# A transformer block on one core: the second half's x turned in 32x32 blocks on VectorE instead of by TensorE

## The chip, the cores and the metric

One core of a Trainium2 chip runs the whole program. The metric is the device time in microseconds (us), median of several runs. Everything is in 32-bit floats; TensorE multiplies in its float32r form, and each operand is split into a high part and a low remainder, so that one product is three matmuls (high x high, high x low, low x high).

## The reference

```python
x = A_x                                          # [1, 2048, 1024]
h = x + _A_ref(_layernorm(x), A_wqkv, A_w_phi, A_wo)
h2 = h + _B_ref(_layernorm(h), B_w1, B_w2)       # relu MLP, 1024 -> 3584 -> 1024

def _A_ref(x, wqkv, w_phi, wo):                  # 32 heads of 32
    q, k, v = ...                                # x @ wqkv, cut into heads
    pq = einsum("bhsd,hdf->bhsf", q, w_phi);  pk = einsum("bhsd,hdf->bhsf", k, w_phi)
    phi_q = concat([softmax(pq), softmax(-pq)]); phi_k = concat([softmax(pk), softmax(-pk)])
    kv = einsum("bhsf,bhsd->bhfd", phi_k, v);  z = phi_k summed over s
    o = (phi_q @ kv) / (phi_q @ z + 1e-6)
    return o @ wo
```

## The kernel before

**Tiles and halves.** The 2048 tokens are 16 tiles of 128, in two halves of eight (HT = 8). In a first part the weight w_phi is folded into the q and k weights; the folded weights are stored in DRAM as `wpk` (k, four sets of 256 columns) and `wpq` (q, two sets of 512 columns). Then comes a list of items, in an order that is the order of TensorE. An item is one tile against one set of weights: eight steps, one for each block of 128 input features, three matmuls of 512 columns a step. For each half the list has four kv slabs (set s = 0 to 3, each over eight tiles; columns are 256 of folded k and 256 of v) and then two q slabs (set s = 0 and 1, eight tiles each). After the second half follow attention, the output projection, and the MLP by a scheme with seven products for eight.

**x in its turned form.** For an item TensorE needs the normalised x with features on the partitions. A tile is held as `xT[t]`, [128, 2, 8, 128]: high and low part, eight feature blocks, 128 tokens. There are eight such buffers, so tile t of the second half takes the buffer of tile t - 8, once the last q item of that tile is done: item `q_n[1, t - 8] + 1`. With `turn = 8 * n + 1` for that item n, tile 8 has turn 329 and each further tile comes eight steps later, tile 15 at 385. The first kv slab of the second half begins at step 384 and takes tile 8 first.

For a tile of the second half, the statistics are computed early, from a load of its own (key `("s", t)`, steps 80 to 211), and scale and bias stay in `scx`. Then x is loaded once more with one DMA (`ln_load`, tokens on the partitions, 4 KB rows), normalised by ScalarE at turn - 8 (`ln_norm`, line 243), and turned in two halves at turn and turn + 3 (`ln_turn`): four TensorE transposes into a PSUM bank (line 250), ScalarE copies the high part out (line 177), VectorE subtracts for the low part (line 178).

**The order of the other work.** `when(step, f, ...)` and `do(item, step, f, ...)` put each piece of side work at a step of the item list; within a step pieces go in the order in which they were registered. Each engine, and each queue that issues DMAs (SP, and ScalarE's for `ed`), executes its instructions in the order that this gives, so an instruction that waits holds up all behind it on its engine.

**Weights.** The class `Units` streams weight blocks. A unit is one feature block of one set: for kv, two DMAs of 128 KB (lines 338, 339), for q one of 256 KB (line 342), into one of six raw buffers; then ScalarE copies the high part (line 124) and VectorE or POOL subtracts for the low part (line 128), into one of ten ring buffers. A slab uses eight units, so two units of the next slab can be split early, and units 2 to 7 are split during the last item of a slab, as its own units come free. A raw buffer that comes free is at once filled with a unit of the slab after.

**Other side work in the same stretch.** Blocks of the MLP weights are loaded (`b`, line 368), combined by four POOL subtractions (line 378) and stored (line 381), all on SP's queue for the DMAs. After each q item VectorE forms the exponents (lines 559 to 563), ScalarE takes the exponential (line 567) and stores it to `ed` from its own queue (line 569).

Of the kernel before, what the change touches and what calls it, by code (L numbers as in the profile page):

```python
# [9 lines left out]
F32 = mybir.dt.float32  # L10
F32R = mybir.dt.float32r
AF = mybir.ActivationFunctionType
ALU = mybir.AluOpType
AX = mybir.AxisListType

P = 128
S = 2048
D = 1024
# [3 lines left out]
NT = S // P  # L22
HT = NT // 2
NK = D // P
# [115 lines left out]
def kernel(  # L140
# [12 lines left out]
    v, act, pool, pe, sp = nc.vector, nc.scalar, nc.gpsimd, nc.tensor, nc.sync  # L153

    consts = ctx.enter_context(tc.tile_pool(name="consts", bufs=1))
    wraw = ctx.enter_context(tc.tile_pool(name="wraw", bufs=RR))
    wring = ctx.enter_context(tc.tile_pool(name="wring", bufs=RW))
    lnp = ctx.enter_context(tc.tile_pool(name="lnp", bufs=2))
    dram = ctx.enter_context(tc.tile_pool(name="scratch", bufs=1, space=bass.MemoryType.DRAM))
# [12 lines left out]
    def f32(ap):  # L172
        return ap.bitcast(F32)
# [14 lines left out]
    def do(n, k, f, *args):  # L188
        at[n, k].append((f, args))

    wpk = [dram.tile([NK, P, 256], F32, name=f"wpk{s}") for s in range(4)]
    wpq = [dram.tile([NK, P, 512], F32, name=f"wpq{s}") for s in range(2)]
# [2 lines left out]
    place_of = {t: (b, i) for b, tiles in enumerate(groups) for i, t in enumerate(tiles)}  # L195
    ed = [dram.tile([P, 8, 4, 256], F32, name=f"ed{b}") for b in range(4)]
    hd = [dram.tile([P, D], F32, name=f"hd{t}") for t in range(NT)]

# [6 lines left out]
    xin, xst, xnt = {}, {}, {}  # L207

    def ln_load(key, parts):
        xin[key] = xlp.tile([P, D], F32, name="xl") if key[0] == "x" and key[1] >= HT and key[1] % 4 > 1 else \  # L210
            lnp.tile([P, D], F32, name="xin")
        n = D // len(parts)
        for j, p in enumerate(parts):
            sp.dma_start(xin[key][:, j * n:(j + 1) * n], p)

    def ln_stats(key):
        src = xin[key]
        st = lnp.tile([P, 2, 6], F32, name="st", bufs=4)
        for j in range(2):
            v.bn_stats(out=st[:, j, :], in_=src[:, j * 512:(j + 1) * 512])  # L220
        mv = lnp.tile([P, 2], F32, name="mv", bufs=4)
        v.bn_aggr(out=mv, in_=st)
        xst[key] = mv
# [14 lines left out]
        v.tensor_scalar(xn[:, 512:D], src[:, 512:D], sc[:, 0:1], sc[:, 1:2], op0=ALU.mult, op1=ALU.add)  # L238

    def ln_norm(key):  # L240
        sc, src = xst.pop(("s", key[1]) if key[0] == "x" and key[1] >= HT else key), xin.pop(key)
        xnt[key] = src if key[0] == "h" else fp_ln.tile([P, D], F32, name="xn")
        act.activation(xnt[key], src, AF.Identity, bias=sc[:, 1:2], scale=sc[:, 0:1])

# [21 lines left out]
    fp_ln = kps.enter_context(tc.tile_pool(name="xn", bufs=2, side="right"))  # L266
# [66 lines left out]
    def load(key, t):  # L333

        kind = key[0]
        if kind == "kv":
            _, hf, s, k = key
            sp.dma_start(t[:, 0:256], wpk[s][k])
            sp.dma_start(t[:, 256:512], wv[s, k])
        elif kind == "q":  # L340
            _, _, s, k = key
            sp.dma_start(t, wpq[s][k])
        elif kind == "wo":
            _, hf, c = key
            sp.dma_start(t, wo[hf, c])
        elif kind == "a":
            sp.dma_start(t, ad[key[1:]])
        else:
            _, _, m, p = key
            w = 1 if kind == "w1" else 2  # L350
            sp.dma_start(t, block(w, p, *{1: (0, 0), 2: (1, 0), 3: (1, 1)}[m]) if m < 4
                         else td[w, p][:, {5: 0, 7: 3 - w, 4: w, 6: 3}[m], :])

    def block(w, p, r, c):

        return w1[2 * p + c, r] if w == 1 else w2[2 * p + r, c]
# [89 lines left out]
    xT = {}  # L446
# [492 lines left out]
    def x_part(t):  # L939
        return [x[t * P:(t + 1) * P, :]]  # L940
# [6 lines left out]
    def when(step, f, *args):  # L947

        if step < 8 * first_up:
            do(step // 8, step % 8, f, *args)  # L950
        else:
            do(first_up + (step - 8 * first_up) // 4, step % 4, f, *args)
# [4 lines left out]
    for t in range(1, NT):  # L957
        n = t - 1 if t < HT else q_n[1, t - HT] + 1
        turn = 8 * n + 1
        if t < HT:  # L960
            stages = X_STEPS.get(t, (turn - 22, turn - 12, turn - 9, turn - 6, turn, turn + 3))
        else:

            early = 80 + 16 * (t - HT)
            when(early, ln_load, ("s", t), x_part(t))
            when(early + 14, ln_stats, ("s", t))
            when(early + 14, xin.pop, ("s", t))
            when(early + 19, ln_power, ("s", t))
            load_ = turn - 88 + 8 * (t - HT) if t < HT + 4 else turn - 36
            stages = (load_, None, None, turn - 8, turn, turn + 3)  # L970
        for step, f, *args in zip(stages, (ln_load, ln_stats, ln_power, ln_norm), [("x", t)] * 4):
            if step is not None:
                when(step, f, *args, *([x_part(t)] if f is ln_load else []))
        do(n, 0, x_open, t)
        for j in range(2):
            when(stages[4 + j], ln_turn, ("x", t), j, lambda t=t: xT[t])


# [5 lines left out]
    for p, n in zip(range(1, 8), (3, 9, 13, 17, 21, 25, 29)):  # L984
        step = 8 * n + (4 if p > 1 else 7)
# [126 lines left out]
    def up_step(b, p, m):  # L1112

        return up0 + 4 * (up_n[b, p, m] + 1 - first_up)

    for j, m in enumerate(UP):

        for g in range(2):
            step = up0 + (8 * j + (-62, -32)[g] if j < 4 else 6 * (j - 4) + 10 + 2 * g)
# [4 lines left out]
            step = up_step(0, NP - 1, m) + 3 * j  # L1124
# [4 lines left out]
    for b in range(2):  # L1129
        for p in range(NP):  # L1130
            for m, k, f, *args in UP_BESIDE:
                if f is up_store:
                    args = [b, p, *args]
# [18 lines left out]
    for b in range(2):  # L1152
        for m in DOWN:
            n = down_n[b, m, NP - 1] + 1
            name, more = {1: "x1", 5: "x4", 6: "x2", 4: "x3"}.get(m), \
# [10 lines left out]


    W = Units(nc, wraw, wring, load, ready, steps)
    half = consts.tile([P, 1], F32, name="half")
    pool.memset(half, -0.5)  # L1170
    eps = consts.tile([P, 1], F32, name="eps")
    pool.memset(eps, DEN_EPS / 2)
    act.activation(consts.tile([P, 1], F32, name="first"), half, AF.Exp)
    scx = consts.tile([P, HT, 2], F32, name="scx")
    consts.tile([P, 56], F32, name="fill")
    ln_load(("x", 0), [x[0:P, 0:512], x[0:P, 512:1024]])
    wt_load(0, sp, slice(0, 512))
    for k in (0, 2):
# [141 lines left out]
```

## Time and profile before

| | |
|---|---|
| median of 3 runs | 1881.68 us (1880.31 to 1882.74) |
| the profiled run | 1881.49 us |
| span of its profile | 1879.7 us |
| busy: TensorE / weight loads | 1872.6 / 1540.3 us |
| busy: VectorE / ScalarE / POOL | 1063.6 / 741.0 / 976.9 us |
| DMA | 433.21 MB, mean 230 GB/s |
| granted TensorE clock | 1.00 |

The profile is one execution. A row of the list of groups gives line, engine, operation, output <- input, how many, then busy time in us and mean ns of one, then the idle time before them and what ended it. A row of the chain gives start and length in us of a piece of the chain of work that ended last. A row of the waits gives who waited for whom, us in total, times, longest. PE is TensorE, PEld its weight loads, DVE VectorE, ACT ScalarE, SPq and ACTq the DMA-issuing parts of SP and ScalarE.

### The profile page before, as it was taken

How to read it: one execution, taken by the hardware profiler on the slowest of the kernel's cores; microseconds unless marked ns; L12 is line 12 of the kernel's file. 1: busy time of each engine (PE TensorE's matmuls, PEld its weight loads, DVE VectorE, ACT ScalarE, POOL GpSimd, SP SyncE). 2: the span in 40 equal slices, each digit the busy share in tenths (PEclk: the TensorE clock that was granted, in tenths of full speed). 3: DMA queues.
4: the chain of work that ended last, by engine and by line, in shares of the span. 5: the costliest groups of instructions: out<-in, count | busy, mean ns of one | idle time of the engine just before them, and what ended most of it. 6: DMA issues, size and time to landing. Idle time of an engine off the chain costs nothing.

```text
span 1879.7 us, 31869 instructions
## 1 busy us (share of the span) xinstructions
PE 1872.6 (100%) x11630; PEld 1540.3 (82%) x11630; DVE 1063.6 (57%) x1714; ACT 741.0 (39%) x1264; POOL 976.9 (52%) x956
## 2 busy tenths in 40 slices
PE   9999999999999999999999999999999999999999
PEld 7888888888888888888888888888888888888887
DVE  7788688677789777455444664444433333343333
ACT  5322244222233122355455554444444444444442
POOL 3778733677745988223343234445444444444443
PEclk9999999999999999999999999999999999999999
DMA  6889875454475567886877997877877677777775
GB/s 214 268 280 312 269 262 180 148 155 141 140 232 190 203 216 237 264 254 209 263 233 241 312 297 248 264 246 259 275 239 216 201 230 239 237 213 220 216 215 177
DMA packets 293036, 433.21 MB, mean 230 GB/s; under 512 B 24208, under 2 KB 150160, under 8 KB 292880
## 3 DMA queue, kind: packets, MB, share of 16 engines
q1 hardware_dynamic: 263712, 390.26, 65.3%
q10 hardware_dynamic: 29168, 40.93, 6.5%
q8 instruction: 91, 1.49, 0.3%
q14 instruction: 65, 0.53, 0.1%
HBM read 293.73 MB, written 137.36 MB: 229 GB/s over the span
## 4 chain that ended last, share of the span: by engine, by line
PE 98%; DVE 1%; ACT 0%; POOL 0%; DMA 0%; issue 0%; SPq 0%; DVEq 0%; POOLq 0%
PE mm L181 25%; PE mm L182 25%; PE mm L183 25%; PE ac L181 4%; PE ac L182 4%; PE ac L183 4%; PE tp L182 2%; PE tp L181 2%; PE tp L183 2%; PE tp L250 1%; PE tp L678 1%; PE ac L491 1%; PE ac L678 1%; PE tp L297 0%; DVE st L220 0%; PE tp L758 0%
## 5 line engine op out<-in xcount | busy, mean ns | idle before, releaser
L128 POOL TENSOR_TENSOR w<-raw,w 128x512 fp32r<-128x512 f32 x353 | 474.6, 1347 | 671.5 <-ACT w L124 638.0
L124 ACT ACTIVATE w<-raw 128x512 fp32r<-128x512 f32 x686 | 409.1, 626 | 491.8 <-PE mm L183 238.9
L128 DVE TENSOR_TENSOR w<-raw,w 128x512 fp32r<-128x512 f32 x333 | 275.0, 827 | 512.9 <-ACT w L124 507.3
L181 PE MATMUL mm<-w,xT 128*128 128x512 f32 x752 | 299.4, 398 | 0.0
L183 PE MATMUL mm<-w,xT 128*128 128x512 f32 x752 | 293.1, 390 | 0.0
L182 PE MATMUL mm<-w,xT 128*128 128x512 f32 x752 | 293.0, 390 | 0.0
L181 PE MATMUL mm<-hT,w 128*128 128x512 f32 x672 | 262.6, 391 | 0.0
L183 PE MATMUL mm<-hT,w 128*128 128x512 f32 x672 | 261.6, 389 | 0.0
L182 PE MATMUL mm<-hT,w 128*128 128x512 f32 x672 | 261.5, 389 | 0.0
L378 POOL TENSOR_TENSOR b<-b 128x256 f32<-128x256 f32 x168 | 129.0, 769 | 85.2 <-DMA b<-in_w_dram 75.4
L181 PEld LDWEIGHTS mm<-w,xT 128*128 128x128 f32 x752 | 141.2, 188 | 31.4 <-issue 2.2
L183 PEld LDWEIGHTS mm<-w,xT 128*128 128x128 f32 x752 | 141.2, 188 | 30.0
L182 PEld LDWEIGHTS mm<-w,xT 128*128 128x128 f32 x752 | 141.3, 188 | 28.5 <-issue 1.0
L181 PE MATMUL mm<-w 128*128 128x512 f32 x392 | 152.5, 389 | 0.0
L182 PE MATMUL mm<-w 128*128 128x512 f32 x392 | 152.5, 389 | 0.0
L183 PE MATMUL mm<-w 128*128 128x512 f32 x392 | 152.5, 389 | 0.0
L183 PEld LDWEIGHTS mm<-hT,w 128*128 128x128 f32 x672 | 126.1, 188 | 26.5
L181 PEld LDWEIGHTS mm<-hT,w 128*128 128x128 f32 x672 | 126.2, 188 | 25.8
L182 PEld LDWEIGHTS mm<-hT,w 128*128 128x128 f32 x672 | 126.2, 188 | 25.7
L480 POOL TENSOR_TENSOR zacc<-zacc,kphi 128x512 f32<-128x512 f32 x60 | 83.8, 1397 | 14.3 <-DVE kphi L472 14.3
L181 PEld LDWEIGHTS mm<-w 128*128 128x128 f32 x392 | 73.6, 188 | 15.3
L182 PEld LDWEIGHTS mm<-w 128*128 128x128 f32 x392 | 73.6, 188 | 15.3
(173 smaller groups left out, 3183.1 us busy)
## 6 DMA issues: line engine op xcount, KB each, us to landing
raw<-t SPq DMA_DIRECT2D x224, 256.0 KB, 4.0
raw<-ad SPq DMA_DIRECT2D x196, 256.0 KB, 3.0
raw<-in_w_dram SPq DMA_DIRECT2D x168, 256.0 KB, 3.2
ad<-c SPq DMA_DIRECT2D x112, 256.0 KB, 4.2
b<-in_w_dram SPq DMA_DIRECT2D x42, 512.0 KB, 5.7
t<-b SPq DMA_DIRECT2D x42, 512.0 KB, 3.6
ad<-s SPq DMA_DIRECT2D x84, 256.0 KB, 4.6
ed<-qe ACTq DMA_DIRECT2D x32, 512.0 KB, 3.9
```

What stands on the lines that cost most here:

```text
L124: nc.scalar.activation(w[:, 0, :], raw[1], AF.Copy)
L128: eng.tensor_tensor(out=w[:, 1, :], in0=raw[1], in1=w[:, 0, :].bitcast(F32), op=ALU.subtract)
L181: pe.matmul(ps, a_hi, b_hi, start=first, stop=False, skip_group_check=more)
L182: pe.matmul(ps, a_hi, b_lo, start=False, stop=False, skip_group_check=more)
L183: pe.matmul(ps, a_lo, b_hi, start=False, stop=last, skip_group_check=more)
L250: pe.transpose(pt[:, k, :], xn[:, (4 * j + k) * P:(4 * j + k + 1) * P], ident)
L378: pool.tensor_tensor(out=tsum[j, *out], in0=tsum[j, *a], in1=tsum[j, *b], op=ALU.subtract)
L480: pool.tensor_tensor(out=zacc[s], in0=zacc[s], in1=phi_of[key], op=ALU.add)
L491: pe.matmul(kv_ps[s][g][32 * i:32 * (i + 1), 0:64], vt[:, 32 * h:32 * (h + 1)], phi[:, 64 * h:64 * (h + 1)], start=first, stop=last)
L678: pe.matmul(banks[g][32 * c:32 * (c + 1), r * P:(r + 1) * P], kvL[rows, 4 * q + 2 * sd + h // 4, 32 * (h % 4):32 * (h % 4 + 1)], phT[rows, ...
```

## The change

Tiles 8 to 15 are no longer turned by TensorE. VectorE's transpose turns each 32x32 block where it stands. So that blocks turned in place give features on the partitions, x is loaded in another layout (`x_load`, four DMAs a tile): partition 32a + j holds, for each group g of 32 tokens, token 32g + j and the 256 features of quarter a. After the turn, feature block k has the features 256a + 32k + f on partition 32a + f, that is 32 rows from each quarter; the second half's kv and q weights are loaded with their rows in that order (`rows_of`). Four tokens share a partition, so norm and bias are needed once for each group: `x_stats` sends `scx` through DRAM (`sxd`) into `srx`, and the norm is four ScalarE instructions of 256 columns (`turn_norm`). High and low part then come from SBUF: one ScalarE copy (`x_high`) and two POOL subtractions (`x_low_part`). The pieces stand at other steps: norm at turn - 11, block transpose at turn - 6, high part at turn, low parts at turn + 2 and turn + 4.

```diff
     def ln_load(key, parts):
-        xin[key] = xlp.tile([P, D], F32, name="xl") if key[0] == "x" and key[1] >= HT and key[1] % 4 > 1 else \
-            lnp.tile([P, D], F32, name="xin")
+        xin[key] = lnp.tile([P, D], F32, name="xin")
...
+    def x_load(t):
+
+        xin["x", t] = (xlp if t % 4 > 1 else lnp).tile([P, D], F32, name="xl" if t % 4 > 1 else "xin")
+        src = x[t * P:(t + 1) * P, :].rearrange("(g j) (a f) -> g a j f", g=4, a=4)
+        for g in range(4):
+            sp.dma_start(xin["x", t][:, 256 * g:256 * (g + 1)], src[g])
+
+    def x_stats(step):
+
+        if step == 0:
+            sp.dma_start(sxd, scx.rearrange("p t c -> p (t c)"))
+            return
+        src = sxd.rearrange("(g j) c -> j g c", g=4)
+        for a in range(4):
+            sp.dma_start(srx[32 * a:32 * (a + 1)], src)
+
+    def turn_norm(dst, src, scale, bias):
+
+        for g in range(4):
+            c = slice(256 * g, 256 * (g + 1))
+            act.activation(dst[:, c], src[:, c], AF.Identity, bias=bias(g), scale=scale(g))
+
+    def x_norm(t):
+        src = xin.pop(("x", t))
+        xnt["x", t] = xn = fp_ln.tile([P, D], F32, name="xn")
+        turn_norm(xn, src, lambda g: srx[:, g, 2 * (t - HT):2 * (t - HT) + 1],
+                  lambda g: srx[:, g, 2 * (t - HT) + 1:2 * (t - HT) + 2])
+
+    def x_turn(t):
+        xn = xnt["x", t]
+        v.transpose(xn, xn)
+
+    def x_parts(t):
+        return [xT[t][:, s].rearrange("p k (g j) -> p k g j", g=4) for s in range(2)], \
+            xnt["x", t].rearrange("p (g k j) -> p k g j", g=4, k=NK)
+
+    def x_high(t):
+        (hi, _), xn = x_parts(t)
+        act.activation(hi, xn, AF.Copy)
+
+    def x_low_part(t, j):
+        (hi, lo), xn = x_parts(t)
+        k = slice(4 * j, 4 * j + 4)
+        pool.tensor_tensor(out=lo[:, k], in0=xn[:, k], in1=f32(hi[:, k]), op=ALU.subtract)
+        if j == 1:
+            del xnt["x", t]
...
         if kind == "kv":
             _, hf, s, k = key
-            sp.dma_start(t[:, 0:256], wpk[s][k])
-            sp.dma_start(t[:, 256:512], wv[s, k])
+            sp.dma_start(t[:, 0:256], rows_of(wpk[s], hf, k))
+            sp.dma_start(t[:, 256:512], rows_of(wv[s], hf, k))
         elif kind == "q":
-            _, _, s, k = key
-            sp.dma_start(t, wpq[s][k])
+            _, hf, s, k = key
+            sp.dma_start(t, rows_of(wpq[s], hf, k))
...
+    def rows_of(w, hf, k):
+
+        return w[k] if hf == 0 else w.rearrange("(a c) p f -> a (c p) f", a=4)[:, 32 * k:32 * (k + 1), :]
...
             load_ = turn - 88 + 8 * (t - HT) if t < HT + 4 else turn - 36
-            stages = (load_, None, None, turn - 8, turn, turn + 3)
+            when(load_, x_load, t)
+            if t == NT - 1:
+                when(early + 24, x_stats, 0)
+                when(early + 34, x_stats, 1)
+            for step, f, *args in ((-11, x_norm), (-6, x_turn), (0, x_high), (2, x_low_part, 0), (4, x_low_part, 1)):
+                when(turn + step, f, t, *args)
+            stages = ()
...
         do(n, 0, x_open, t)
-        for j in range(2):
+        for j in range(2 if t < HT else 0):
             when(stages[4 + j], ln_turn, ("x", t), j, lambda t=t: xT[t])
...
-    half = consts.tile([P, 1], F32, name="half")
+    small = consts.tile([P, 8], F32, name="small")
+    half, eps = small[:, 0:1], small[:, 1:2]
...
     scx = consts.tile([P, HT, 2], F32, name="scx")
-    consts.tile([P, 56], F32, name="fill")
+    srx = consts.tile([P, 4, 2 * HT], F32, name="srx")
+    consts.tile([P, 8], F32, name="fill")
```

More of the change, by code (lines that the diff above doesn't have):

```diff
@@ L197 @@
     hd = [dram.tile([P, D], F32, name=f"hd{t}") for t in range(NT)]
+    sxd = dram.tile([P, 2 * HT], F32, name="sxd")
     hs = {(b, m): dram.tile([P, 4, 512], F32, name=f"hs{b}_{m}") for b in range(2) for m in UP}
@@ L240, in ln_norm @@
     def ln_norm(key):
-        sc, src = xst.pop(("s", key[1]) if key[0] == "x" and key[1] >= HT else key), xin.pop(key)
+        sc, src = xst.pop(key), xin.pop(key)
         xnt[key] = src if key[0] == "h" else fp_ln.tile([P, D], F32, name="xn")
@@ L1168 @@
     W = Units(nc, wraw, wring, load, ready, steps)
-    half = consts.tile([P, 1], F32, name="half")
+    small = consts.tile([P, 8], F32, name="small")
+    half, eps = small[:, 0:1], small[:, 1:2]
     pool.memset(half, -0.5)
-    eps = consts.tile([P, 1], F32, name="eps")
     pool.memset(eps, DEN_EPS / 2)
-    act.activation(consts.tile([P, 1], F32, name="first"), half, AF.Exp)
+    act.activation(small[:, 2:3], half, AF.Exp)
     scx = consts.tile([P, HT, 2], F32, name="scx")
-    consts.tile([P, 56], F32, name="fill")
+    srx = consts.tile([P, 4, 2 * HT], F32, name="srx")
+    consts.tile([P, 8], F32, name="fill")
     ln_load(("x", 0), [x[0:P, 0:512], x[0:P, 512:1024]])
```

## The prediction

> **What bounds the kernel now.** I read the page's busy line and its chain first, then the waits of TensorE, then the stretch in which the second half's x is turned.
>
> ```profile
> span 1879.7 us, 31869 instructions
> PE 1872.6 (100%) x11630; PEld 1540.3 (82%) x11630; DVE 1063.6 (57%) x1714; ACT 741.0 (39%) x1264; POOL 976.9 (52%) x956
> PE 98%; DVE 1%; ACT 0%; POOL 0%; DMA 0%; issue 0%; SPq 0%; DVEq 0%; POOLq 0%
> ...
> PE tp L1193 <- POOL ones L1189: 1.6, 1, 1.6
> PE tp L1212 <- ACT xn L237: 1.2, 1, 1.2
> ...
> L250 PE MATMUL tp<-ident,xn x64: 270/272/273, 266.9 to 314.5; 128*128 128x128 f32 x64
> ...
> 267.03 0.44 PE tp L250 x4
> ...
> 311.18 0.23 PE mm L181
> ...
> 311.87 0.44 PE tp L250 x4
> ```
>
> TensorE is the chain (98%); its longest waits for others are 1.6 and 1.2 us, both in the opening (lines 1193 and 1212). So work taken off it is saved whole, as long as nothing new comes late; and anything that comes late for it is lost whole, since there is no idle time to soak it up. The 64 transposes of tiles 8 to 15 stand in the chain as 16 groups of four, 0.44 us each, from 267 to 314.5 us, between matmuls of 0.23.
>
> **What the change takes away.** 16 x 0.44 = 7.0 us of TensorE. That is all that can be won: 1881.5 - 7.0 = 1874.5 us (the profiled run took 1881.49 us, 1.8 over its span and 0.2 under the median of 1881.68, so I count from 1881.5 and put nothing on for the difference). It is 0.37%; about 0.2%, 3.8 us, is what a measurement of this kernel can tell from no change.
>
> **What it adds to the other engines, per tile of x.**
>
> ```profile
> L664 DVE STREAM_TRANSPOSE qe<-qe 128x1024 f32<-128x1024 f32 x28 | 34.2, 1227 | 12.1 <-POOL qe L658 9.5 <-POOL qe L648 1.7 <-DMA xh<-in_x_dram 1.0
> L567 ACT ACTIVATE qe<-qe 128x1024 f32<-128x1024 f32 x32 | 33.9, 1061 | 61.0 <-DVE qe L563 51.6 <-DMA qe<-ed 9.3
> L453 ACT ACTIVATE vt<-mm 128x256 f32<-128x256 f32 x64 | 24.5, 382 | 125.0 <-PE mm L183 125.0
> L128 POOL TENSOR_TENSOR w<-raw,w 128x512 fp32r<-128x512 f32 x353 | 474.6, 1347 | 671.5 <-ACT w L124 638.0
> L178 DVE TENSOR_TENSOR xT<-tp,xT 128x512 fp32r<-128x512 f32 x30 | 20.3, 678 | 6.1 <-ACT xT L177 6.1
> L177 ACT ACTIVATE xT<-tp 128x512 fp32r<-128x512 f32 x30 | 17.9, 597 | 33.2 <-PE tp L250 33.1
> L243 ACT ACTIVATE xn<-xl,scx 128x1024 f32<-128x1024 f32 x4 | 4.9, 1234 | 0.0
> L378 POOL TENSOR_TENSOR b<-b 128x256 f32<-128x256 f32 x168 | 129.0, 769 | 85.2 <-DMA b<-in_w_dram 75.4
> ...
> 205.00:258.00 53.00, 53.00 (x294) 43.73 (x293) 38.93 (x69) 15.96 (x24) 29.48 (x31) 1.00 0.78 258
> 258.00:284.00 26.00, 26.00 (x127) 21.50 (x126) 24.34 (x35) 15.35 (x20) 9.10 (x9) 1.00 0.83 270
> 284.00:315.00 31.00, 31.00 (x157) 25.61 (x156) 25.91 (x41) 17.34 (x25) 10.02 (x11) 1.00 0.54 176
> 315.00:545.00 230.00, 230.00 (x1484) 187.64 (x1483) 166.98 (x324) 65.97 (x117) 150.96 (x147) 1.00 0.50 156
> ```
>
> (The last four lines are stretches: length, then busy time of TensorE, its weight loads, VectorE, ScalarE and POOL, the granted clock, the share of the 16 DMA engines, GB/s.) VectorE loses two subtractions (2 x 0.68) and gains one block transpose priced as that of line 664 (1.23): -0.1. ScalarE loses 1.23 + 2 x 0.60 and gains four norms of 256 columns (as line 453, 0.38 each) and one copy of 1024 (as line 567, 1.06): 2.6 for 2.4, +0.2. POOL gains two subtractions of 1.35: 2.7, or 21.6 over eight tiles; between 258 and 315 us it is busy 19.1 of 57, so this fits and would cost its 21.6 only if POOL had no idle time. The scale bounce adds five small transfers on SP, the last of them 92 steps (of three matmuls, 0.69 us) before the first norm that reads them: 63 us of projections hide it, and it would cost one landing, some 4 us, without them. The constants only change places: nothing. The normalised tile is now kept until POOL's second subtraction, and the norm of the tile two later (ScalarE, one step behind) waits for that, with weight splits and q's exponentials queued behind it: one POOL instruction, 1.35, covered by those POOL gaps, and 4.5 if the four sums of a weight block (line 378, 4 x 0.77) stand ahead.
>
> **What it does to the transfers.** This decides the case. Loads of x, and of the second half's kv and q weights, now have a source that counts four blocks outermost (a, 256 features apart), then 32 rows, then the run; before, 128 rows were outermost on both sides. The DMA answer for 260 to 281 us:
>
> ```profile
> DMA packets 5610, 6.55 MB, mean 312 GB/s; under 512 B 371, under 2 KB 5229, under 8 KB 5609
> q10 hardware_dynamic: 1973, 1.97, 27.9%
> issues: line engine op xcount, KB each, median us to landing
> ed<-qe ACTq DMA_DIRECT2D x4, 512.0 KB, 4.5
> xin<-in_x_dram SPq DMA_DIRECT2D x2, 512.0 KB, 4.5
> raw<-wpk SPq DMA_DIRECT2D x7, 128.0 KB, 4.0
> raw<-in_wv_dram SPq DMA_DIRECT2D x7, 128.0 KB, 3.7
> b<-in_w_dram SPq DMA_DIRECT2D x1, 512.0 KB, 5.3
> t<-b SPq DMA_DIRECT2D x1, 512.0 KB, 5.7
> xl<-in_x_dram SPq DMA_DIRECT2D x1, 512.0 KB, 5.9
> ```
>
> 23 issues and 371 tiny packets: 16 for each (368) that close it. So a transfer is dealt to 16 engines in 16 shares, each with its own close. A share has to be the same bytes on both sides; with 128 rows outermost on both, 16 shares of eight rows are a plain cut. With four blocks outermost on one side the plain cut gives four shares, on four engines, and the other twelve stand by. No row shows such a transfer, so the two ends are 16 shares (nothing changes) and four. I take four, since all that the trace shows is a cut of the outermost count.
>
> The Trainium skill, page "DMA: Bandwidth & Descriptors", section "Why a DMA increments its semaphore by 16 and not by 1", states this as a rule: a hardware queue uses the largest number of engines up to 16 that divides the slowest dimension of both patterns, and the lowest-numbered ones. By that rule it is four here, and always the same four; the trace agrees so far only in that every 128-row transfer closes 16 times. With that rule the sum below is 1910 us; if sixteen engines take part all the same, 1874.5.
>
> Price: q10 carries only 1 KB rows (stores of ed). 27.9% of 16 engines x 21 us is 93.7 us, over 1973 packets less some 60 closes: 49 ns per KB. A tile of x is 512 KB: 32 KB on each of 16 engines, 1.6 us, or 128 KB on each of four, 6.3: +4.7. A kv unit (128 KB twice) is 0.8 or 3.1: +2.35.
>
> Which loads pile up:
>
> ```profile
> L214 SPq DMA_DIRECT2D xin<-in_x_dram x4: 448/563/1206, 205.2 to 275.2; - x4
> L214 SPq DMA_DIRECT2D xl<-in_x_dram x4: 328/439/929, 220.4 to 282.1; - x4
> ...
> 258.28 0.33 SPq L338 DMA_DIRECT2D raw<-wpk  x1
> ...
> 273.55 0.57 SPq L338 DMA_DIRECT2D raw<-wpk  x1
> ...
> 304.87 0.63 ACT L124 ACTIVATE w<-raw 128x512 fp32r<-128x512 f32 x1 [1.28 <-PE mm L183]
> ...
> 306.43 1.23 ACT L243 ACTIVATE xn<-xl,scx 128x1024 f32<-128x1024 f32 x1
> ...
> 305.58 1.29 POOL L128 TENSOR_TENSOR w<-raw,w 128x512 fp32r<-128x512 f32 x1 [14.70 <-ACT w L124]
> 310.30 1.81 POOL L128 TENSOR_TENSOR w<-raw,w 128x512 fp32r<-128x512 f32 x1 [0.22 <-DMA raw<-in_wv_dram]
> ```
>
> All eight x tiles are issued between 205 and 282 us (three more issues of about 0.5 each, 12 us on SP in 77: no price, as SP mostly waits for buffers), and between 258 and 274 the eight units of the first kv slab of the half. Before, an engine has 0.78 x 53 + 0.83 x 26 = 62.9 us of work from 205 to 284. On the four engines come 8 x 4.7 + 8 x 2.35 = 56.4. Together 119.3 us: tile 15, the last of them, lands no sooner than 205 + 119.3 = 324, and with ed stores from the other queue taking turns (one per 5.3 us by the 260 to 281 answer, seven until then, of which I count four, since the exponentials behind the waiting norms don't come: 4 x 32 x 0.049 = 6.3) at about 331.
>
> Who waits: the norm of tile 15 ran at 306.4, just behind the split of unit 2 of the coming slab (304.9). The change moves it three steps ahead (turn - 11 for turn - 8), in front of that split on the in-order ScalarE. So units 2 to 7 now wait for tile 15: 331 + 4 x 0.38 norms + 1.06 exponential + 0.63 split = 334. On POOL the sums of the weight blocks loaded right behind tile 15 come first (they land at 331 + 1.6 and take 4 x 0.77, with one x subtraction of 1.35 between), 337, then unit 2's low half, 1.3: 338.5. TensorE needs unit 2 two steps into the slab's first item. The transposes at 311.87 stand one step (three matmuls of 0.23) into that item, so it needed unit 2 at 313.0 before, and at 306 if the 7.0 us are saved. It stands still until 338.5: the run is 338.5 - 313.0 = 25.5 us longer than before, the saving included.
>
> Later, each kv slab has eight units, 8 x 2.35 = 19 us more on the four engines in eight items of 5.5, 44 us, whose share was 0.50, 22: 41 of 44, just under full. Loads run almost a slab ahead, so the weights themselves are in time; the block loads behind them come some 10 us later, and POOL with its sums. I take 1 us for each of the three slab changes that follow, between 0 and 4 each. Sum: 1881.5 + 25.5 + 3 = 1910 us.
>
> Ends of that case: without ed stores between (6.3) and without the block sums ahead on POOL (4.1) the stall is 25.5 - 10.4 = 15 us, and with nothing later that gives 1896.5; I put the end at 1890, since a denser packing of the packets than 49 ns may be had with twelve engines still. If SP, blocked by block stores that wait for late block loads, issues the slab's loads 8 us later (a block load's 5.3 and its four sums), and each slab change costs 4: 1881.5 + 33.5 + 12 = 1927, and 1932 for the q weights that follow.
>
> **Rivals.**
> Sixteen shares: the source is dealt out row by row after all. The 368 closes speak for the number 16, nothing speaks for how. Then landing stays near 4 us and the loads are as early as before. What is left is POOL at the slab's opening: unit 6's low half ended at 310.30 + 1.81 = 312.1 and was needed at 316.2 (six steps of 0.69 and two groups of 0.44 after 311.2); two subtractions of tile 14, 2.7, come in front of it, and 4.1 holds them. So 1874.5, up to 1877 if a block sum falls in between too. This ends on the other side. It decides as soon as a 128-row transfer with four blocks outermost closes 16 times.
> Four shares, but hidden: the norms wait, yet TensorE goes on with four banks in hand. For it: q's first operations are VectorE's, and three items of 24 matmuls, 5.5 us each, can be in flight. Against it: units 2 to 7 stand behind the norm, whatever the banks do. It needs tile 15 some 20 us sooner, by 310; then the stall is about the size of the saving: 1881.
> POOL alone: 16 shares, and 21.6 us of subtractions that cost as much as they take at full load. Against it the 19.1 busy of 57. Were a third of it exposed, 7.2, it would undo the saving: 1881.7.
>
> **Chances.** Four shares and a late tile 15: 0.78, all slower, own range 1890 to 1932. Sixteen shares: 0.14, faster. Hidden, or undone by POOL: 0.08, of which 0.06 within 0.2% and the rest split between the sides. So faster 0.15, same 0.06, slower 0.79. The time is that of the first, 1910; as its own range holds it with about 0.65, the whole range goes down to the sixteen-share case, 1874.
>
> **What would show it.** Right: tiny packets (under 512 B) fall between 260 and 281 us although there are more issues; x loads take well over 6 us to land; ScalarE's norm of tile 15 waits for DMA; TensorE shows a wait for a weight split of 20 us and more near 306; line 250's 64 transposes between 267 and 315 us are gone. Wrong: 16 closes for each of the new loads, landing near 4 us, and TensorE without waits, which gives 1874.5; or four closes and TensorE without waits, which would mean that my pile of work is too high.

## The result, and the profile after

The changed kernel takes 1948.99 us (median of four runs, 1948.48 to 1951.79) against 1880.99 for the kernel before (median of four): 1.0364 times as long (95% interval 1.0348 to 1.0381), 68 us. The forecast was 1910, with 1932 as its upper end. The direction was right, the size was not.

The page of the changed kernel:

```profile
span 1947.0 us, 31804 instructions
PE 1881.6 (97%) x11566; PEld 1538.5 (79%) x11566; DVE 1059.3 (54%) x1706; ACT 745.2 (38%) x1280; POOL 997.4 (51%) x972
...
DMA packets 295869, 433.26 MB, mean 223 GB/s; under 512 B 23968, under 2 KB 154016, under 8 KB 295712
...
PE 79%; DMA 7%; POOL 6%; issue 3%; DVE 3%; SPq 2%; ACT 1%; ACTq 0%; POOLq 0%; DVEq 0%
```

The 64 transposes are gone (11630 - 11566), and TensorE's share of the chain has fallen from 98% to 79%: DMA, POOL and the issuing of DMAs now stand in it. Idle time of TensorE rose from 1879.7 - 1872.6 = 7.1 us to 65.4, that is 58.3; the other 9.0 of the 67.3 that the span grew are busy time, although 7.0 us of work were taken away.

TensorE's waits after (who waited for whom, us in total, times, longest), then stretches of the same run (length; busy time of TensorE, weight loads, VectorE, ScalarE, POOL; granted clock, DMA share, GB/s):

```profile
PE mm L182 <- POOL w L128: 14.1, 6, 8.0
PE mm L181 <- ACT w L124: 14.1, 1, 14.1
PE mm L181 <- DVE qe L614: 11.1, 3, 9.1
PE tp L569 <- POOL zacc L531: 8.8, 2, 4.5
```

```profile
205.00:267.00 62.00, 59.54 (x320) 48.47 (x319) 42.88 (x73) 19.81 (x30) 33.50 (x33) 1.00 0.71 230
267.00:310.00 43.00, 33.35 (x145) 26.68 (x143) 20.93 (x29) 16.32 (x25) 12.20 (x11) 0.95 0.42 144
310.00:345.00 35.00, 17.71 (x54) 12.73 (x55) 24.59 (x33) 18.43 (x27) 19.32 (x18) 0.72 0.44 146
345.00:572.00 227.00, 200.25 (x1245) 158.22 (x1243) 133.71 (x274) 53.33 (x102) 133.57 (x133) 0.95 0.39 125
```

The loss lies between 205 and 572 us. The granted clock falls where TensorE idles, to 0.72 from 310 to 345, so an idle stretch also makes the matmuls in and behind it longer: busy time came to 1881.6 where 1872.6 - 7.0 = 1865.6 was due, 16 us more. By the trace's clock records, half the clock was granted for 47.8 us between 305 and 565 us, and TensorE was busy in 26.1 of them; at the full clock that work takes 13 us less. The other 3 us are not explained. (The Trainium skill, page "TensorE: Matmul & The Clock Gate", section "Part 1: The HAM clock gate (the "warmup" mystery)", states that the clock halves after an idle window; the trace agrees, as its records from 305 to 565 us hold no value but 1.0 and 0.5, and 0.72 is their mean over one stretch.)

Where the lag builds up, read from the trace at TensorE's first kv sum in each kv slab of the second half, at the first of its last group of kv sums, and at the start of attention (kv sums are TensorE's `ac<-kphi,vt`, line 491 before and 542 after):

| us | slab 0 | slab 1 | slab 2 | slab 3 | last | attention |
|---|---|---|---|---|---|---|
| before | 342.0 | 389.4 | 436.7 | 484.1 | 507.1 | 548.5 |
| after | 369.1 | 433.0 | 491.0 | 542.2 | 572.3 | 613.6 |
| lag | 27.1 | 43.6 | 54.3 | 58.1 | 65.2 | 65.1 |

So there are two parts: 27 us up to the first slab, for which the forecast had 25.5, and 38 us more in the kv slabs, for which it had 3.

**Four shares.** The page before had this row, and the DMA answer of the changed kernel for 260 to 281 us these:

```profile
DMA packets 293036, 433.21 MB, mean 230 GB/s; under 512 B 24208, under 2 KB 150160, under 8 KB 292880
```

```profile
GB/s 390 236 222 351 343 100 18 72 98 96 137 263 359 287 144 285 386 353 107 64 78 101 94 98 98 94 96 99 125 98 98 94 98 98 94 98 98 94 98 259
DMA packets 3378, 3.37 MB, mean 160 GB/s; under 512 B 104, under 2 KB 3377, under 8 KB 3377
```

Tiny packets fell from 24208 to 23968. With four closes for each of the 80 weight loads and 32 x loads in place of 16 for each of 88, five scale transfers of 16 and their 640 small pieces, it comes out to the packet: 24208 - 1408 + 448 + 80 + 640 = 23968. So the rule that the prediction took from the Trainium skill, page "DMA: Bandwidth & Descriptors", section "Why a DMA increments its semaphore by 16 and not by 1" (the largest number up to 16 that divides the slowest dimension of both patterns), holds here. From about 271 us on, nearly all slices stand at 94 to 99 GB/s: four engines at some 24.5 GB/s each, 1 KB in 42 ns (49 in the forecast).

**The queues.** Issues on SP between 315 and 545 us, first of before, then of after (count; ns shortest/median/longest):

```profile
L338 SPq DMA_DIRECT2D raw<-wpk x18: 326/352/448, 318.9 to 413.3; - x18
...
L339 SPq DMA_DIRECT2D raw<-in_wv_dram x19: 422/431/493, 314.8 to 413.6; - x19
```

```profile
L385 SPq DMA_DIRECT2D raw<-wpk x24: 509/1217/2135, 336.4 to 468.8; - x24
...
L386 SPq DMA_DIRECT2D raw<-in_wv_dram x24: 536/1276/2139, 337.0 to 470.1; - x24
```

By the medians a kv unit used to hold SP for 0.35 + 0.43 = 0.78 us, and now holds it for 1.22 + 1.28 = 2.49. Summed over all 64 kv loads of the second half in the trace, the issues take 74.1 us in place of 27.8: 46.3 more, 11.6 per slab, on the queue that also issues the MLP's block loads. A batch of units and the block load in line behind them, from the SP timeline:

```profile
392.83 0.56 SPq L385 DMA_DIRECT2D raw<-wpk  x1
...
395.31 0.51 SPq L385 DMA_DIRECT2D raw<-wpk  x1
395.87 1.03 SPq L386 DMA_DIRECT2D raw<-in_wv_dram  x1
396.94 1.69 SPq L385 DMA_DIRECT2D raw<-wpk  x1
398.68 1.28 SPq L386 DMA_DIRECT2D raw<-in_wv_dram  x1
...
405.28 1.24 SPq L419 DMA_DIRECT2D b<-in_w_dram  x1
```

The first five issues of the batch are short; from the sixth on they take 1.0 us and more. Counted from the landing records, for the 48 kv loads that SP issues between 315 and 545 us: with up to four DMAs still on their way when it begins, an issue takes 0.51 to 0.63 us (15 of 15), with five or six 1.03 to 2.14 (33 of 33). And 128 KB at 98 GB/s are 1.34 us, so these issues come at about the pace at which four engines empty.

POOL's wait for the blocks over 315 to 545 us (us, times), first before, then after, more than doubled:

```profile
  DMA b<-in_w_dram: 33.9, 10
```

```profile
  DMA b<-in_w_dram: 73.4, 11
```

POOL's sums stand ahead of its weight splits and of `zacc`, which is what TensorE waits for in the rows above (14.1 and 8.8). The chain of the changed kernel between 345 and 550 us, by share, says the same: block loads and POOL's sums lead it, and a weight load itself has 7%.

```profile
by line: DMA b<-in_w_dram 31.7%; POOL b L429 18.1%; issue 17.5%; DMA raw<-in_wv_dram 7.0%; POOL zacc L531 6.1%; POOL w L128 3.1%; DVE w L128 3.0%; POOL xl L651 2.3%; ACT w L124 1.5%; SPq L432 1.4%; SPq L385 1.3%; DVE xtz L656 1.2%; DVE ksm 
```

**A loop of ScalarE and POOL.** ScalarE and POOL of after, in order of time (start, length):

```profile
318.63 1.06 ACT L254 ACTIVATE xT<-xn 128x1024 fp32r<-128x1024 f32 x1 [0.50 <-ACT qe L618]
322.31 2.07 ACT L236 ACTIVATE xn<-xl,srx 128x256 f32<-128x256 f32 x4 [2.62 <-POOL xT L259]
324.29 1.04 ACT L618 ACTIVATE qe<-qe 128x1024 f32<-128x1024 f32 x1
325.36 0.37 ACTq L620 DMA_DIRECT2D ed<-qe  x1
325.83 1.06 ACT L254 ACTIVATE xT<-xn 128x1024 fp32r<-128x1024 f32 x1 [0.50 <-DVE xn L246]
```

```profile
319.76 2.51 POOL L259 TENSOR_TENSOR xT<-xn,xT 128x512 fp32r<-128x512 f32 x2 [4.70 <-ACT xT L254]
```

The high part of tile t (line 254), POOL's two low parts (line 259), the norm of tile t + 2 (line 236), the exponential, the store's issue and the high part of tile t + 1 follow one another, each waiting for the last: 325.83 - 318.63 = 7.20 us for a tile, where a q item takes TensorE 5.5. The norm at turn(t + 2) - 11 is turn(t) + 5, one step behind the low part at turn(t) + 4, and there are two `xn` buffers.

**The other queue.** ScalarE's exponential, and the issue of the store behind it:

```profile
269.50 1.04 ACT L618 ACTIVATE qe<-qe 128x1024 f32<-128x1024 f32 x1
279.64 0.37 ACTq L620 DMA_DIRECT2D ed<-qe  x1
280.13 0.63 ACT L124 ACTIVATE w<-raw 128x512 fp32r<-128x512 f32 x1 [9.59 <-DMA raw<-wpk]
```

Nothing on ScalarE ran for 9 us. The semaphore records of the trace show why: the DMAs of both queues take eight semaphores in turn, and an issue first waits until the DMA that had its semaphore before has landed; here that is a weight load issued at 270.08, which landed at 279.56. Slow loads, and four of them for one, hold the other queue too: nine of the 16 stores of this half start within 0.1 us of such a landing in after, none in before. The long issues of SP in the kv slabs are something else: for all 88 issues of SP between 315 and 545 us that earlier DMA had landed at least 1.4 us before the issue began.

### The profile page after: what moved, and what is told of

Its sections match the earlier page's. It is cut to its first block, busy times and chain, and to the rows that moved or that the text cites. A ratio compares the mean times of both kernels' runs of the same rounds, so it can differ in the third digit from the quotient of the medians.

```text
span 1947.0 us, 31804 instructions
## 1 busy us (share of the span) xinstructions
PE 1881.6 (97%) x11566; PEld 1538.5 (79%) x11566; DVE 1059.3 (54%) x1706; ACT 745.2 (38%) x1280; POOL 997.4 (51%) x972
## 4 chain that ended last, share of the span: by engine, by line
PE 79%; DMA 7%; POOL 6%; issue 3%; DVE 3%; SPq 2%; ACT 1%; ACTq 0%; POOLq 0%; DVEq 0%
PE mm L181 19%; PE mm L182 19%; PE mm L183 19%; DMA b<-in_w_dram 4%; PE ac L181 4%; PE ac L183 4%; PE ac L182 4%; POOL b L429 2%; PE tp L182 2%; PE tp L181 2%; PE tp L183 2%; DMA raw<-in_wv_dram 1%; POOL w L128 1%; PE tp L729 1%; PE tp L297 1%
## 5 line engine op out<-in xcount | busy, mean ns | idle before, releaser
L181 PE MATMUL mm<-w,xT 128*128 128x512 f32 x752 | 303.4, 403 | 25.2 <-ACT w L124 14.1
L182 PE MATMUL mm<-w,xT 128*128 128x512 f32 x752 | 298.8, 397 | 22.1 <-POOL w L128 14.1
L183 PE MATMUL mm<-w,xT 128*128 128x512 f32 x752 | 296.6, 394 | 0.0
L181 PEld LDWEIGHTS mm<-w,xT 128*128 128x128 f32 x752 | 143.9, 191 | 60.7 <-issue 15.0
L182 PEld LDWEIGHTS mm<-w,xT 128*128 128x128 f32 x752 | 143.8, 191 | 58.6 <-POOL w L128 19.1
L183 PEld LDWEIGHTS mm<-w,xT 128*128 128x128 f32 x752 | 143.7, 191 | 29.8
L515 ACT ACTIVATE ke<-ke 128x512 f32<-128x512 f32 x64 | 40.4, 631 | 149.0 <-DVE ke L511 149.0
L181 PEld LDWEIGHTS mm<-w 128*128 128x128 f32 x392 | 73.6, 188 | 15.3
```

The lines of the kernel that those rows point to most:

```text
L181: pe.matmul(ps, a_hi, b_hi, start=first, stop=False, skip_group_check=more)
L182: pe.matmul(ps, a_hi, b_lo, start=False, stop=False, skip_group_check=more)
L183: pe.matmul(ps, a_lo, b_hi, start=False, stop=last, skip_group_check=more)
L515: act.activation(e_of[key], e_of[key], AF.Exp)
```

## The experiments

The theories at the outset. A: everything comes from the four shares; with 16, 1874.5. B: x's work at its new places and on its new engines has a price of its own; after e1 this was narrowed to the loop of ScalarE and POOL (theory D, or "loop", in the texts from e5 on). C: what counts is how long SP and the places in flight are held, not how the bytes are spread (A2 in the text of e4). Another rival, called C in the texts of e2 and e8: scattered rows as such are slow.

### e1 to e4: which loads, and which of their properties

x in 16 shares (e1, e2, e4): the same 4 KB per partition, but split by partitions. Outermost are 32 rows on both sides.

```diff
-        src = x[t * P:(t + 1) * P, :].rearrange("(g j) (a f) -> g a j f", g=4, a=4)
-        for g in range(4):
-            sp.dma_start(xin["x", t][:, 256 * g:256 * (g + 1)], src[g])
+        src = x[t * P:(t + 1) * P, :].rearrange("(g j) (a f) -> a j g f", g=4, a=4)
+        for a in range(4):
+            sp.dma_start(xin["x", t][32 * a:32 * (a + 1), :].rearrange("j (g f) -> j g f", g=4), src[a])
```

Weights in 16 shares (e1, e3): whole blocks as before; feature block k has the features 8n + k in both halves, the weights come from the host in that order, and norms and transposes read with a stride of 8.

```diff
-        return w[k] if hf == 0 else w.rearrange("(a c) p f -> a (c p) f", a=4)[:, 32 * k:32 * (k + 1), :]
+        return w[k]
...
+            act.activation(dst[:, c].rearrange("p (k f) -> p k f", k=NK),
+                           src[:, c].rearrange("p (f k) -> p k f", k=NK), AF.Identity, bias=bias(g), scale=scale(g))
```

e4 has x as in e1, and each weight load of the change as four DMAs of 32 partitions (`rows_of(w, hf, k)[a]`): 16 engines for each, but four times the issues.

e1, both in 16 shares. 

> The changed kernel with every load dealt to 16 engines: x by four DMAs of 32 partitions (source 32 tokens outermost), the kv and q weights in whole blocks of 128 rows again, since the order of features is now 8n + k in both halves (input arrays laid out so, first-half transposes and the norms read with a stride of 8). Theory A, four engines: all late transfers are gone and the 7 us of transposes are saved: 1874.5 us (1872 to 1878), no waits of TensorE between 200 and 600 us. Rival B, the new places and engines of x's work (norm ahead of the weight splits, 16 more POOL subtractions, scale bounce) cost: still 1900 or more.

e2, x alone. 

> The changed kernel with x alone dealt to 16 engines; the second half's weights still come in four shares. Theory A: tile 15 lands some 38 us earlier, so the first stall (27 us by the opening of the second half's first kv slab) goes to about -5, and the 10 us of each kv slab stay: 1881 - 5 + 38 = 1914 us (1900 to 1925). Theory A with x as the whole cause: about 1880. Rival C, the scattered rows as such are slow to read, not the dealing: x's source rows are the same 1 KB runs, so 1949 as before the edit.

e3, weights alone. 

> The changed kernel with the weights in whole blocks again (feature order 8n + k in both halves), x still in four shares. Theory A: the kv slabs are as long as in the kernel before (47 us instead of 57); the pile ahead of tile 15 is 62.9 + 37.6 = 100.5 us from 205 us on, so it lands near 312, some 10 us late: 1881 - 7 + 10 = 1884 us (1876 to 1895). Rival B: 1930 or more, since x's work stands where it stood.

e4, 16 engines, four times the issues. 

> x dealt to 16 engines and each weight load of the second half cut into four DMAs of 32 partitions, which are dealt to 16 engines each: the data spreads, but SP issues four times as many. Theory A1, what counts is the load on four engines and the late landing: about 1876 us (1873 to 1885). Theory A2, what counts is the time that SP is held by the issues (1.3 us for each four-share load, against 0.33 to 0.43 before; here four issues of about 0.33 each, 1.3 again): the kv slabs stay some 8 to 10 us longer, about 1905 us (1895 to 1915).

Measured: e1 1897.28 us (ratio 1.0085, 1.0071 to 1.0099), e2 1934.35 (1.0282, 1.0263 to 1.0300), e3 1899.97 (1.0099, 1.0080 to 1.0117), e4 1950.10 (1.0365, 1.0346 to 1.0384). None came out as expected: e1 lies between its two forecasts, and e2, e3 and e4 lie 9, 5 and 35 us above the upper ends of theirs. A falls with e1: with 16 shares everywhere the run is still 16 us longer than before, all of it ahead of the first slab (first kv sum at 357.6, +15.6; later slabs as long as before), in one wait of 16.7 us of TensorE for ScalarE's split. The weights carry most of the loss: e1 and e3, which have whole blocks, lie at 1897 and 1900, and e2, which has not, at 1934.

e4 speaks for C. Its SP row over 315 to 545 us:

```profile
L406 SPq DMA_DIRECT2D raw<-wpk x96: 325/419/1451, 326.3 to 480.2; - x96
L406 SPq DMA_DIRECT2D raw<-in_wv_dram x96: 310/419/1550, 328.0 to 482.0; - x96
```

A unit is eight issues of 0.42, 3.35 us of SP, and the kv slabs lose some 49 us although the bytes lie on all engines. So four overloaded engines aren't needed for the loss; a queue that is held is enough. The places in flight are not what holds it: of SP's 256 issues between 315 and 545 us only four begin within 0.15 us of the landing of the DMA that had their semaphore before. SP's own time is: the kv loads of the second half take 114 us of issuing in place of 27.8.

### e5, e6, e9: the loop

One edit takes the norm out of the loop, three steps later, so that the norm of tile t + 2 comes behind the high part of tile t + 1 on ScalarE and POOL's next low parts don't wait for it:

```diff
-            for step, f, *args in ((-11, x_norm), (-6, x_turn), (0, x_high), (2, x_low_part, 0), (4, x_low_part, 1)):
+            for step, f, *args in ((-8, x_norm), (-6, x_turn), (0, x_high), (2, x_low_part, 0), (4, x_low_part, 1)):
```

e6 is the changed kernel with that edit alone. e5 has it together with 16 shares for x (as e1) and whole weight blocks in the change's own feature order: the weights come from the host with the rows of block k as 256a + 32k + f, for both halves, and the first half's norms write their output by block, so that the second half's norms and the transposes read without a stride. e9 is e5 with turn - 11.

```diff
+    def by_block(xn):
+        return xn.rearrange("p (k a f) -> p a k f", a=4, k=NK)
...
-        "wqkT": wqkv[:, :2 * D].T.reshape(16, P, D),
+        "wqkT": wqkv[:, :2 * D].T.reshape(2 * D, 4, NK, 32).transpose(0, 2, 1, 3).reshape(16, P, D),
```

e5. 

> All loads dealt to 16 engines (x by four DMAs of 32 partitions; weights in whole blocks of 128 rows, the feature order 256a + 32k + f now in both halves, written by the first half's norms), and the norm of x at turn - 8 in place of turn - 11, so that it no longer waits on ScalarE for POOL's subtraction of the tile two before. Theory D (two causes: four shares, and the loop ScalarE - POOL - ScalarE through the two xn buffers, which turns a tile every 8.3 us where an item takes 5.4): both are gone, 1874.5 us (1872 to 1878). Rival B, POOL's 16 more subtractions or other work of x's new path hold TensorE: 1885 or more.

e6. 

> The changed kernel with one number changed: the norm at turn - 8 for turn - 11. Theory D: the loop is gone, the four shares stay: the first stall shrinks from 27 us to 5 or 10, the kv slabs keep their 38: 1927 us (1918 to 1935). If the loop is no cause with four shares (all is late landing): 1945 or more.

e9. 

> The 1876.3 us kernel (16 shares for x and for the weights, contiguous norms) with the norm put back from turn - 8 to turn - 11, nothing else. Theory loop (the norm one step ahead of the low part of the tile two before it makes ScalarE and POOL wait for each other, some 7 us per tile against 5.45 per item, paid once at the first slab): first mark some 14 us later than with turn - 8, slabs unchanged, 1876.3 + 14 = about 1890 (1885 to 1896), with one TensorE wait for ScalarE's weight split of 12 to 17 us. Rival (the loop only bites because the norms of the earlier 16-share kernel read strided, 8.3 us per tile): 1876 to 1880, no such wait.

Measured: e5 1876.26 us (ratio 0.9965, 0.9953 to 0.9977), a little faster than the kernel before; e9 1890.19 (1.0047, 1.0030 to 1.0065); e6 1938.26 (1.0299, 1.0280 to 1.0318), 11 us above what was expected of it: its first kv sum comes 17.0 us late where 5 to 10 was expected, while its slabs lose 37.5, as forecast. ScalarE of e9, two tiles running, and TensorE's longest wait there; then TensorE's longest in e5:

```profile
294.29 2.08 ACT L236 ACTIVATE xn<-xin,srx 128x256 f32<-128x256 f32 x4 [2.66 <-POOL xT L259]
...
301.54 2.08 ACT L236 ACTIVATE xn<-xl,srx 128x256 f32<-128x256 f32 x4 [2.66 <-POOL xT L259]
```

```profile
PE mm L181 <- ACT w L124: 10.8, 1, 10.8
```

```profile
PE tp L1259 <- POOL ones L1255: 1.6, 1, 1.6
```

In e9 the loop turns in 301.54 - 294.29 = 7.25 us with every load landing early, so it needs no late transfer: the loop is shown to cost by itself, and its price is 1890.2 - 1876.3 = 13.9 us. The wait that was expected at 12 to 17 us is 10.8. Strided norms made the loop slower in e1 (there norms start 8.3 us apart), and e1 lies 7.1 above e9, 8.0 at the first kv sum. In e5 TensorE has no wait over 1.6 us, and that one stands in the opening as before.

### e10, e11: one cost at a time, without the loop

Both have the norm at turn - 8. e10 is the changed kernel with x in 16 shares, so only the weights' cost is left; e11 is e5 with x loaded as in the change, so only x's is.

e10. 

> The changed kernel with x in 16 shares and the norm at turn - 8; the second half's weights stay in four shares. It leaves only the weights' cost. Theory (weights in four shares hold SP's queue and everything in flight, some 10 us at each of the four kv slabs; the loop costs 14 and x little): 1934.4 - 14 = 1920 (1910 to 1927), kv slabs some 10 us longer each, no wait of 10 us at the first slab. Rival (late x and the loop were what made the later slabs late too): under 1895.

e11. 

> The 1876.3 us kernel with x loaded in four shares as in the change, weights in 16 shares, norm at turn - 8. It leaves only x's cost. Theory (x in four shares alone is hidden or nearly: the pile ahead of tile 15 needs the kv units on the same engines): 1876 to 1884, TensorE waits under 6 us in all. Rival (x in four shares alone is late, as the prediction's own pile less the units would have it, 119.3 - 18.8 = 100 us of work from 205, landing at 306 to 312, some 10 us late for the split): 1886 to 1892.

Measured: e10 1924.20 us (1.0219, 1.0175 to 1.0263), as its theory had it, and e11 1887.43 (1.0037, 1.0025 to 1.0048). With the rest this gives all corners but one (the kernel before took 1880.9 to 1881.7 beside them):

| x | weights | norm | us |
|---|---|---|---|
| 16 shares | 16 shares | turn - 8 | 1876.3 (e5) |
| 16 | 16 | turn - 11 | 1890.2 (e9) |
| four | 16 | turn - 8 | 1887.4 (e11) |
| 16 | four | turn - 8 | 1924.2 (e10) |
| 16 | four | turn - 11 | 1934.4 (e2) |
| four | four | turn - 8 | 1938.3 (e6) |
| four | four | turn - 11 | 1949.0 (the change) |

Alone, weights in four shares cost 47.9 us, x in four 11.2, the early norm 13.9; together 73.0, and the change lies 72.7 above e5. That the sum fits so closely is luck: in pairs the costs differ by up to 4 us (weights 44.2 beside the early norm, 50.9 beside x in four; the early norm 10.2 and 10.7 beside the weights). The corner that is missing, four, 16 and turn - 11, was run only with strided norms: e3 lies just 2.7 above e1, so most of x's cost is hidden where the loop is late already.

e11 went to the rival: x in four shares isn't hidden. Lines of the chain in e11 between 270 and 345 us, by share, and SP's x loads there:

```profile
by line: DMA b<-in_w_dram 26.3%; POOL b L437 19.0%; SPq L221 15.5%; DMA t<-b 9.8%; POOL xT L259 8.9%; POOL w L128 8.0%; issue 7.0%; SPq L394 2.7%; SPq L393 2.0%; POOL zacc L539 1.8%; SPq L440 0.7%; POOLq L128 0.2%; POOLq L437 0.0%
```

```profile
283.89 11.93 SPq L221 DMA_DIRECT2D xl<-in_x_dram  x8
295.86 3.92 SPq L427 DMA_DIRECT2D b<-in_w_dram  x2
```

Eight issues of x hold SP for 12 us, the block loads behind them go out at 296 and land late (DMA `b` is the largest share of that chain), and POOL's sums of them run into the splits. ScalarE's queue is held as well: in e11 its stores stood four times for a slow load's semaphore, 9.6 us in all, and the norm of tile 15 starts at 310.5 where in e5 it starts at 300.5. It isn't the norm of x that waits for its tile; it is what stands behind x on the queues.

### e7, e8, e12: the weights alone, on the kernel before

The second half's kv and q weights are loaded as four blocks of 32 rows (e7), eight of 16 (e12) or 16 of eight (e8) in the kernel before. These rows don't fit the order of x's features, so the second half's products are of other rows; the amount of work is as it was.

```diff
+    def rows_of(w, hf, k):
+        return w[k] if hf == 0 else w.rearrange("k p f -> (k p) f").rearrange("(a r) f -> a r f", a=4)[:, 32 * k:32 * (k + 1), :]
```

e7. 

> The kernel before, with the second half's kv and q weights loaded as four blocks of 32 rows (a row order that doesn't fit its x, so the second half's projections are those of rows out of order); nothing else is changed, x goes through TensorE. Theory A: the four kv slabs get about 9 us longer each, 1881 + 36 = 1917 us (1908 to 1925). If the slabs' loss comes from x's new path: 1881.

e8. 

> As the run before, but 16 blocks of 8 rows: the source is scattered more finely, and still 16 blocks are outermost (same remark on the rows' order). Theory A: 16 shares, 1881 us (1879 to 1884). Rival C, scattered rows as such are slow: at least the 1917 of four blocks.

e12. 

> The kernel before with the second half's kv and q weights loaded as eight blocks of 16 rows each (the rows do not fit x's feature order, so the products are of other rows; the work is the same). A dose between four blocks (1924.5) and 16 (1885.8). Theory (what costs is the time that a load holds its engines and the queue; at eight shares a unit is 1.6 us instead of 3.1, and the engines have room again): 1882 to 1893. Rival (any cut that is not 16 makes each issue slow, whatever the load of the engines): 1905 to 1925. Packets under 512 B: 24208 - 80 x 8 = 23568 if there are eight shares.

Measured: e7 1924.52 us (1.0226, 1.0207 to 1.0244), e12 1889.69 (1.0040, 1.0023 to 1.0057), e8 1885.80 (1.0022, 1.0012 to 1.0032). Tiny packets are 23248, 23568 and 24208: 4, 8 and 16 closes a load. SP's issues of line 338 in e7, e12 and e8, in that order:

```profile
L338 SPq DMA_DIRECT2D raw<-wpk x22: 510/1178/2065, 315.2 to 443.8; - x22
```

```profile
L338 SPq DMA_DIRECT2D raw<-wpk x18: 577/579/800, 319.6 to 417.4; - x18
```

```profile
L338 SPq DMA_DIRECT2D raw<-wpk x18: 514/540/597, 317.4 to 413.7; - x18
```

With whole blocks it was 352. Against the kernel before beside them, e7 loses 42.8 us, e12 8.8 and e8 4.1: the weights' cost doesn't need the change at all, and it isn't in proportion. e7 and e12 lie in the ranges of their theories, e8 2 us above its own; as e8 scatters the rows most finely and loses least, scattered rows as such are not the cause. At 16 and at eight shares the issue costs 0.2 us more and that hardly varies (shortest and median are nearly the same); at four the shortest is still 0.51, but the median is 1.18. Here too it hangs on the DMAs under way: with five and more, 31 of 34 kv issues of e7 take over 1 us, with fewer none of ten; in e12 it is one of 18 with five and more. The cost jumps where this begins. e12 and e8 differ by 4.7 us at nearly the same issue time, so the longer transfers may have a part of their own; no run shows it apart.

## Why the prediction was wrong

- **What is taken away, 7.0 us.** Borne out: e5, without the change's three costs, is faster by a ratio of 0.9965, 5.4 us between the medians (4.3 to 8.8 by its interval). The sixteen-share rival's 1874.5 to 1877 was the right price for a kernel that has 16 shares and the later norm, and not for 16 shares alone (e9: 1890.2).
- **The prices on the engines.** The block transpose took 1.24 us (1.23 forecast), the low part 1.34 (1.35), the high copy 1.05 (1.06). Four norms of a tile take 2.07 for a forecast of 1.5. None of this decides.
- **"One POOL instruction, 1.35, covered": wrong.** The step looked at how busy POOL was, not at what follows what. Norm, exponential, high part and two low parts became one loop of 7.2 us per tile against 5.5 for an item; the cover is gone as soon as the loop is longer than the item. 13.9 us alone (e9 against e5), 10.7 in the change itself (e6).
- **Four shares: right**, to the packet.
- **The stall, 25.5 us: 27.1 measured, for another reason.** Tile 15's norm started at 331, as forecast, but by the landing records its tile was in at 317.7, 13 us before, and the trace names POOL and not a DMA for its wait:

```profile
330.96 2.08 ACT L236 ACTIVATE xn<-xl,srx 128x256 f32<-128x256 f32 x4 [4.08 <-POOL xT L259]
```

  The sign that was to show the step right, a wait for DMA at that norm, is missing, and instead of one wait of 20 us and more near 306 TensorE has one of 14.1 from 321 on, with shorter ones before it. What made the norm late is the loop, two stops of ScalarE at a store's issue (9 us from 270.5 on, 7 from 295.4 on), and SP held by the x loads. The pile of work on the four engines was priced too high (in part by its 49 ns for 1 KB, where 42 were measured). That the sum fits is chance.
- **"Three more of about 0.5 each … no price": wrong.** The 32 x issues have a median of 1.2 us:

```profile
L221 SPq DMA_DIRECT2D xin<-in_x_dram x16: 531/1214/1971, 204.2 to 296.1; - x16
L221 SPq DMA_DIRECT2D xl<-in_x_dram x16: 532/1249/2133, 224.0 to 307.5; - x16
```

  The prediction took an issue's time from rows of 16-share loads. Summed, these are 37.6 us of SP where the eight loads before took 4.9: 32.7 more, for the forecast's 12, in a stretch where it also issues 16 weight loads, most of them at over 1 us.
- **"1 us for each of three slab changes": the term that decided, mis-sized.** It came to 38 us. The forecast weighed the load of the four engines, 41 of 44 us, found it just under full and stopped there. It named the right next thing ("the block loads behind them come some 10 us later, and POOL with its sums") but gave it no price beyond 4 us a slab, since it priced the bytes on the engines and not the time that the queue is held. SP is held 11.6 us longer per slab, 46 in four, and the block loads stand behind it; the weights alone cost 42.8 (e7) to 47.9 (e10).
- **The granted clock** had no term. Some 13 us of the measured time are matmuls at half the clock next to idle time; a stall costs more than its length.

What stays open: what it is that makes a four-share issue wait once five DMAs are under way. In the kv slabs it isn't the eight semaphores (in the changed kernel each had been free for 1.4 us and more); a depth of what lies between SP and the four engines fits, but no run varies it. Open too is how the loss in the slabs divides between SP's held time and block loads that land later on busy engines: e4 shows that the first is enough, not that the second costs nothing.

## What to carry to other kernels

Price a changed DMA three times: the bytes on the engines that it really uses, the time that it holds the queue that issues it, and what stands behind it on that queue; a load at 41 of 44 of its engines' time looked just under full here, and the loss showed at another load, behind it on the queue. When a buffer of two is kept longer, write down the loop of instructions that it closes and compare its length with the item; busy shares say nothing on this. And put a permutation where it is free, on the host or in an instruction that writes anyway: e5 gets the same turn of x with whole-block loads, and wins what the change was worth.

## What the runs showed of the hardware

- A DMA whose outermost count is 4, 8 or 16 closes as often. With four shares the loads ran at some 98 GB/s in all, which fits four engines of 24.5.
- The issue itself gets longer: a median of 0.35 us for a whole block of 128 KB, 0.54 for 16 blocks of eight rows, 0.58 for eight of 16, 1.18 and up to 2.1 for four of 32. With four of 32, in the changed kernel's kv slabs, it is 0.51 to 0.63 us while up to four DMAs are under way and 1.03 to 2.14 with five or six.
- A slow DMA of SP delays issues of ScalarE's queue that take its semaphore next, and with them ScalarE's own work, by 9 us at a store of the changed kernel.
- VectorE turns 128x1024 elements in 32x32 blocks, in place, in 1.24 us.
